# Attention ahead of two expert layers on one core: queries loaded ahead of values in three buffers, a unit's exponents in one instruction, routed transposes on four banks

## The chip, the cores and the metric

The kernel runs on one core of a Trainium2 chip. The metric is device time in microseconds (us), as the median of several runs. Engines are named as in the profile: PE multiplies matrices (PEld loads its weights), DVE, ACT and POOL work on vectors, SP issues most of the transfers (DMAs). Each engine takes its instructions in the order in which the program was written; a waiting instruction holds everything behind it on that engine.

## The reference

Three layers follow one another: attention (2 batches, 8 heads, 768 positions, 64 wide; each query sees a window of 31 keys and 24 block summaries), an expert layer in which every token goes through all 8 experts (weights from Sinkhorn), and one in which each token goes to a single expert.

```python
k_sum = k.reshape(B, H, nb, block, D).max(axis=3)
v_sum = v.reshape(B, H, nb, block, D).mean(axis=3)
scores_l = scale * np.matmul(q, k.transpose(0, 1, 3, 2))
mask_l = np.abs(pos[:, None] - pos[None, :]) < window
scores_s = scale * np.einsum('bhsd,bhnd->bhsn', q, k_sum) + np.log(block)
scores_all = np.concatenate([np.where(mask_l, scores_l, -1e9), scores_s], axis=-1)
a = np.exp(scores_all - np.max(scores_all, axis=-1, keepdims=True))
a = a / (np.sum(a, axis=-1, keepdims=True) + 1e-09)
attn = np.matmul(a, np.concatenate([v, v_sum], axis=2))
...
for e in range(E):                       # dense: every expert sees every token
    out += P[:, e:e + 1] * (np.maximum(x @ w1[e], 0.0) @ w2[e])
...
for e in range(E):                       # routed: a token goes to its best expert
    h = np.maximum(x[mask] @ w1[e], 0.0)
    out[mask] = gate_w[mask, None] * eom[mask, e, None] * (h @ w2[e])
```

## The kernel before

**Units.** Attention is cut into 16 units: a batch b, a half g of its positions (384 queries) and a pair hp of heads. The loop of `steps` runs 18 times; its step i carries out, in the order of the table `STEPS`, one part each of several units: `flip` of unit i-2 (PE transposes the finished weights `e`, L276, and ACT copies them out as `aT`), `scores` of unit i (PE, L220), `transposes_q` of unit i+1 (PE, L97), `means` of i-1, `maxima` of i (DVE: six pairs of instructions at L236 add the mask, write `e` to SBUF and leave the extreme of every row in `mx`), `fill_v` of i-1 (ACT), `exponents` of i (ACT, L249: six instructions of 120 columns, each with a bias from `mx` and a running sum into `sm`), `sum_v` of i (POOL, L128, three additions over the values `vn`), `transposes_k` of i+2 (PE, copies on DVE at L186, a reduction at L190), `apply` of i-2 (PE L289, then DVE makes `xhi`, `xlo`), and at the end `normalise` of i: DVE L258 and L259 turn `sm` into `rs`, POOL multiplies `e` by it (L261, 128x720). Then the step issues loads: a piece of the experts' weights (`raw`, the fillers), keys, queries, values.

**What sets the order.** The instructions of an engine stand as the Python code emits them. PE's first instruction of a step is `flip` of unit i-2, whose `e` was normalised at the end of step i-2: a whole step lies between. The function `merge` puts pieces of the dense layer's matmuls (L603, L623, with `hhi` on ACT and `hlo`, `acc` on DVE) between the parts of the attention from the end of step 6 on; before that attention runs alone, with `warm` matmuls on ones in its first steps. The weights of the dense layer arrive as `raw`; ACT makes `hi` of them (L471) and DVE `lo` (L472, both inputs in SBUF).

**Buffers.** `qn` (queries as loaded) has two buffers, `vn` one, `kn` three. Values of unit i+1 can only be loaded when `sum_v` of unit i is through. Loads of q, k and v all stand in SP's one queue. `whole` says for which head pairs the load takes each head apart, in longer runs; PE then transposes them with six 64-wide matmuls in place of three of 128.

**Routed part.** At the end, tiles of 128 tokens go through `flip_x`, `mm1`, `flip_h` and `mm2` (L1735 to L1772). `flip_h` writes two halves of `h`, transposed, into PSUM banks of role "t", which `flip_x` uses too; there are two such banks. `evac` empties one with ACT (`hi`) and then DVE (`lo`, L1728).

Of the kernel before, what the change touches and what calls it, by code (L numbers as in the profile page):

```python
# [12 lines left out]
ACTF = mybir.ActivationFunctionType  # L13
ALU = mybir.AluOpType
AX = mybir.AxisListType
# [7 lines left out]
class Attention:  # L23
# [10 lines left out]
    LAG = 2  # L34
    STEPS = (
        ("flip", -LAG, 0.65), ("scores", 0, 0.9), ("transposes_q", 1, 0.35),
        ("means", -1, 0.2), ("maxima", 0, 0), ("fill_v", -1, 0), ("exponents", 0, 0),
        ("sum_v", 0, 0), ("transposes_k", 2, 0.7), ("apply", -LAG, 0.95), ("normalise", 0, 0),
    )

    def __init__(self, tc, pool, ident, ones, masks, q, k, v, xhi, xlo, psum):
# [19 lines left out]
    def load_rows(self, src, n, tag, whole, bufs):  # L61

        p = src.shape[1] // n
        shape = [p, 2, n, 64] if whole else [p, n, 2, 64]
        t = self.pool.tile(shape, F32, tag=tag, name=tag, bufs=bufs)
        self.nc.sync.dma_start(  # L70
            out=t, in_=src.rearrange("h (p r) d -> p h r d" if whole else "h (p r) d -> p r h d", r=n)
        )
        return t
# [5 lines left out]

    def load_q(self, b, g, hp):  # L80
        self.qn[b, g, hp] = self.load_rows(
            self.q[b, 2 * hp:2 * hp + 2, 384 * g:384 * g + 384], 3, "qn", self.whole(b, g, hp), 2
        )

    def whole(self, b, g, hp):
        return b == g == 0 and hp < 2

    def transpose_rows(self, tr, rows, r0, whole):
        for r in range(3):
            if whole:  # L90
                for h in range(2):
                    self.nc.tensor.matmul(
                        tr[64 * h:64 * h + 64, r, :], rows[:, h, r0 + r], self.ident,
                        start=True, stop=True,
                    )
            else:
                self.nc.tensor.transpose(  # L97
                    tr[:, r, :], rows[:, r0 + r].rearrange("p h d -> p (h d)"), self.ident
                )
# [128 lines left out]
    def maxima(self, b, g, hp):  # L228
        nc = self.nc
        e, mx, sm = self.an[b, g, hp]  # L230
        for par in range(2):
            sc = self.sc[par]
            for j in range(3):
                qt = 3 * g + j
                m = 0 if qt == 0 else (2 if qt == 5 else 1)
                nc.vector.tensor_tensor_reduce(  # L236
                    out=e[:, par, j], in0=sc[:, j], in1=self.masks[:, m], scale=1.0,
                    scalar=3.0e38, op0=ALU.add, op1=ALU.min,
                    accum_out=mx[:, 3 * par + j:3 * par + j + 1],
                )  # L240

    def exponents(self, b, g, hp):
        e, mx, sm = self.an[b, g, hp]
        for par in range(2):
            if par:
                yield
            for j in range(3):
                i = 3 * par + j
                self.nc.scalar.activation(  # L249
                    out=e[:, par, j], in_=e[:, par, j], func=ACTF.Exp, scale=-1.0,  # L250
                    bias=mx[:, i:i + 1], accum_out=sm[:, i:i + 1],
                )

    def normalise(self, b, g, hp):
        nc = self.nc
        e, _, sm = self.an[b, g, hp]
        rs = self.pool.tile([128, 6], F32, tag="rs", name="rs", bufs=2)
        nc.vector.tensor_scalar(out=sm, in0=sm, scalar1=1.0e-9, scalar2=None, op0=ALU.add)  # L258
        nc.vector.reciprocal(rs, sm)  # L259
        an = e.rearrange("p a j c -> p (a j) c")  # L260
        nc.gpsimd.tensor_tensor(  # L261
            out=an, in0=an,
            in1=rs.unsqueeze(2).to_broadcast([128, 6, 120]), op=ALU.mult,
        )
        self.an[b, g, hp] = an
# [41 lines left out]
    def steps(self, fillers):  # L307

        U, LAG = self.units, self.LAG
        once = ("transposes_k", "means")

        def load(f, i):
            if i < len(U):
                f(*U[i])

        load(self.load_k, 0)
        load(self.load_q, 0)  # L320
        self.make_blocks()
        load(self.load_k, 1)
        load(self.load_q, 1)
        load(self.load_k, 2)
        load(self.load_vn, 0)
        load(self.load_v, 0)
        load(self.load_v, 1)
        self.warm(8)
        yield -LAG
        for _ in self.transposes_k(*U[0]):  # L330
            yield -LAG
        self.transposes_q(*U[0])
        for _ in self.transposes_k(*U[1]):
            yield -LAG
        load(self.load_k, 3)
        load(self.load_q, 2)
        load(self.load_vn, 1)
        yield -LAG
        for i in range(len(U) + LAG):
            parts = [  # L340
                (getattr(self, what), U[i + d], cost if U[i + d][1] == 0 or what not in once else 0)
                for what, d, cost in self.STEPS if 0 <= i + d < len(U)
            ]
            total, at = sum(p[2] for p in parts), 0
            for f, unit, cost in parts:
                n = 0
                for _ in f(*unit) or ():
                    n += 1
                    if cost:
                        yield i - LAG + (at + cost * n / 2) / total  # L350
                at += cost
                if cost and at < total:
                    yield i - LAG + at / total
            if i < 3 + LAG:
                self.warm(8)
            for f in fillers.get(i, ()):
                f()
            load(self.load_k, i + 4)
            load(self.load_q, i + 3)
            load(self.load_vn, i + 2)  # L360
            load(self.load_v, i + 2)
            yield i - LAG + 1
# [24 lines left out]
class DenseMoe:  # L387
# [56 lines left out]
    def load(self, which, hx, c):  # L444
        nc = self.nc
        e, f0 = hx // 2, 512 * (hx % 2)
        t = self.rpool.tile([128, 512], F32, tag="raw", name="raw", bufs=4)
        if self.strassen(hx):

            if which == 1:  # L450
                d, f = 256 * (c % 2), f0 + 256 * (c // 2)
                src = self.w1[e][d:d + 256, f:f + 256]
            else:
                f, d = f0 + 256 * (c // 2), 256 * (c % 2)
                src = self.w2[e][f:f + 256, d:d + 256]
            (nc.gpsimd if hx > self.FIRST else nc.sync).dma_start(
                out=t.rearrange("p (k f) -> p k f", k=2),
                in_=src.rearrange("(k p) f -> p k f", p=128),
            )
        elif which == 2:  # L460
            nc.sync.dma_start(out=t, in_=self.w2[e][f0 + 128 * c:f0 + 128 * c + 128, :])
        else:
            f = f0 + 128 * c
            nc.sync.dma_start(
                out=t.rearrange("p (k f) -> p k f", k=4),
                in_=self.w1[e][:, f:f + 128].rearrange("(k p) f -> p k f", p=128),
            )
        self.raw[which, hx, c] = t
# [1370 lines left out]
def kernel(  # L1839
# [14 lines left out]
    nc = tc.nc  # L1854
# [16 lines left out]
            "zX": (3, 5), "zY": (2,), "zD": (1,),  # L1871
        },
        "routed": {"a": (4,), "b": (5,), "t": (0, 1), "m2": (3, 2), "m1": (6, 7)},
    }
    phase = ["attention"]
    turn = {}
# [14 lines left out]
    def pool(stack, name, side):  # L1891
        return stack.enter_context(
            tc.tile_pool(name=name, bufs=1, side=side, reuse_waits="tile")
        )

    with ExitStack() as stacks:
# [38 lines left out]
        moe2 = RoutedMoe(tc, ident, routing, moe2_w1, moe2_w2, out, psum)  # L1935
# [110 lines left out]
        def until(what):  # L2046
            while what not in finished:
                next(late, None)
# [3 lines left out]
        until("early")  # L2052
        tail_stack.close()
        moe2.begin_rest(pool(tail_stack, "m2b", "right"))
        for _ in moe2.steps(lambda: until("final")):
            next(late, None)


# [29 lines left out]
```

## Time and profile before

| | us |
|---|---|
| median of 3 runs (1327.66 to 1328.57) | 1328.5 |
| profiled execution | 1328.97 |
| its span | 1326.9 |
| PE busy | 1289.9 (97%) |
| DVE busy | 846.2 (64%) |
| ACT busy | 744.4 (56%) |
| POOL busy | 341.9 (26%) |

The span is the time from the first to the last recorded instruction; 2.1 us of the profiled execution's time lie around it. A busy share is a mean over stages; what holds a stage is read from the rows of that stage, by the idle time in front of an instruction and by what ended it.

### The profile page before, as it was taken

What the parts mean: (1) busy time and instruction counts of PE and PEld (TensorE: products, weight loads), DVE (VectorE), ACT (ScalarE), POOL (GpSimd) and SP (SyncE); (2) the same over time, 40 slices, a digit from 0 to 9 for tenths busy, and PEclk for the clock granted to TensorE, in tenths of its full rate; (3) what the DMA queues carried; (4) which work ended last, traced back from release to release, by engine and by line L of the source; (5) the groups of instructions that cost most, each with busy time, mean ns of one, the idle gap of its engine ahead of it and who ended that gap; (6) DMA issues with size and microseconds to landing.
All of it is one profiled execution on the core that took longest, in us unless ns stands there. A gap on an engine that the chain in (4) does not pass through costs nothing. (4 is left out here: it accounts for less than half of the span.)

```text
span 1326.9 us, 27071 instructions
## 1 busy us (share of the span) xinstructions
PE 1289.9 (97%) x10067; PEld 1214.2 (92%) x10067; DVE 846.2 (64%) x1673; ACT 744.4 (56%) x1523; POOL 341.9 (26%) x365
## 2 busy tenths in 40 slices
PE   7899999999999999999999999999999999999995
PEld 7788789999999999999999999999999998788783
DVE  5764587687778787787777786787643358313440
ACT  4875223577677676677677676777632115234451
POOL 4351004333233242333233242332210001111110
PEclk8999999999999999999999999999999999999998
DMA  8761227589789897988898897987661236123440
GB/s 186 163 145 34 95 96 270 176 175 207 190 175 196 194 206 170 224 169 211 189 192 186 188 197 186 216 169 184 94 167 40 80 129 213 49 82 118 168 147 23
DMA packets 167278, 208.90 MB, mean 157 GB/s; under 512 B 52319, under 2 KB 100447, under 8 KB 167136
## 3 DMA queue, kind: packets, MB, share of 16 engines
q1 hardware_dynamic: 118288, 138.36, 33.5%
q0 software_dynamic: 48848, 68.70, 30.2%
q8 instruction: 82, 1.34, 0.4%
q14 instruction: 60, 0.49, 0.1%
HBM read 151.18 MB, written 56.62 MB: 157 GB/s over the span
## 5 line engine op out<-in xcount | busy, mean ns | idle before, releaser
L840 POOL DMA_DIRECT2D x2d<-acc x144 | 172.8, 1242 | 454.0 <-ACT acc L835 214.0
L676 PE MATMUL bank<-hi,hlo 128*128 128x256 f32 x672 | 190.0, 283 | 0.3 <-DVE hlo L711 0.3
L676 PE MATMUL bank<-lo,hhi 128*128 128x256 f32 x672 | 189.9, 283 | 0.0
L676 PE MATMUL bank<-hi,hhi 128*128 128x256 f32 x672 | 189.5, 282 | 0.0
L676 PE MATMUL bank<-Tlo,hi 128*128 128x256 f32 x576 | 162.9, 283 | 0.0
L676 PE MATMUL bank<-Thi,lo 128*128 128x256 f32 x576 | 162.6, 282 | 0.0
L676 PE MATMUL bank<-Thi,hi 128*128 128x256 f32 x576 | 162.1, 281 | 0.0
L676 PE MATMUL bank<-hi,acc 128*128 128x256 f32 x672 | 133.7, 282 | 0.0
L676 PEld LDWEIGHTS bank<-hi,hhi 128*128 128x128 f32 x672 | 127.9, 190 | 0.3 <-DVE acc L860 0.2
L676 PEld LDWEIGHTS bank<-hi,hlo 128*128 128x128 f32 x672 | 127.4, 190 | 0.5 <-DVE hlo L711 0.5
L676 PEld LDWEIGHTS bank<-lo,hhi 128*128 128x128 f32 x672 | 127.4, 190 | 0.0
L676 PE MATMUL bank<-xhi,hi 128*128 128x256 f32 x432 | 121.4, 281 | 0.7 <-ACT t L770 0.7
L676 PE MATMUL bank<-xlo,hi 128*128 128x256 f32 x432 | 121.4, 281 | 0.0
L676 PE MATMUL bank<-xhi,lo 128*128 128x256 f32 x432 | 121.3, 281 | 0.0
L676 PEld LDWEIGHTS bank<-hi,acc 128*128 128x128 f32 x672 | 109.8, 190 | 0.0
L676 PEld LDWEIGHTS bank<-Thi,hi 128*128 128x128 f32 x576 | 109.0, 189 | 0.0
L676 PEld LDWEIGHTS bank<-Thi,lo 128*128 128x128 f32 x576 | 108.6, 189 | 0.0
L676 PEld LDWEIGHTS bank<-Tlo,hi 128*128 128x128 f32 x576 | 108.3, 188 | 0.0
L711 DVE TENSOR_TENSOR hlo<-t,hhi 128x512 fp32r<-128x512 f32 x144 | 97.0, 685 | 14.2 <-ACT hhi L703 13.4
L703 ACT CAST hhi<-t 128x512 fp32r<-128x512 f32 x144 | 88.1, 619 | 23.7 <-DVE t L805 17.3
L610 ACT ACTIVATE hhi<-bank 128x384 fp32r<-128x384 f32 x64 | 31.4, 491 | 120.3 <-PE bank L603 120.1
L835 ACT ACTIVATE acc<-acc,P 128x256 f32<-128x256 f32 x216 | 96.7, 502 | 3.5 <-DVE acc L877 2.7
(311 smaller groups left out, 3463.4 us busy)
## 6 DMA issues: line engine op xcount, KB each, us to landing
x2d<-acc POOLq DMA_DIRECT2D x147, 256.0 KB, 5.1
Thi<-td SPq DMA_DIRECT2D x144, 256.0 KB, 3.6
Tlo<-td SPq DMA_DIRECT2D x144, 256.0 KB, 4.0
raw<-in_moe_w_dram POOLq DMA_DIRECT2D x88, 256.0 KB, 6.0
raw<-in_moe_w_dram SPq DMA_DIRECT2D x20, 1024.0 KB, 6.4
raw<-in_moe_w_dram SPq DMA_DIRECT2D x40, 256.0 KB, 3.9
x2d<-acc SPq DMA_DIRECT2D x21, 256.0 KB, 2.4
kn<-in_k_dram SPq DMA_DIRECT2D x8, 384.0 KB, 4.7
```

The costliest lines, as they stand in the source:

```text
L610: nc.scalar.activation(out=hhi[:, c], in_=ps, func=ACTF.Relu)
L676: self.nc.tensor.matmul(bank[:, 256 * f:256 * f + 256], x[:, o:o + 128], y[:, k], start=first and n == 1, stop=n == 12, skip_group_check=True,
L703: nc.scalar.copy(hi, src)
L711: nc.vector.tensor_tensor(out=lo, in0=src, in1=hi.bitcast(F32), op=ALU.subtract)
L835: nc.scalar.activation(out=out[:, s], in_=src[:, s], func=ACTF.Copy, scale=self.P[:, i, hx // 2:hx // 2 + 1],)
L840: nc.gpsimd.dma_start(out=self.sums[n:n + 256, 256 * dh:256 * dh + 256].rearrange("(c p) d -> p c d", p=128), in_=out.rearrange("p (c d) - ...
```

## The change

`normalise` moves from the end of step i to step i+1, right after `maxima`, and now makes the sums itself (a DVE reduction over `e`). `maxima` ends with a POOL instruction that subtracts `mx` from all of `e`, and `exponents` is one ACT instruction over the whole unit. `qn` gets three buffers, queries are loaded one unit earlier, and in a step's loads they stand ahead of the weights, keys and values. All four head pairs of the first half of batch 0 are loaded head by head. In the routed part the role "t" gets banks 0, 1, 4 and 5 from the point "final" on.

```diff
     STEPS = (
         ("flip", -LAG, 0.65), ("scores", 0, 0.9), ("transposes_q", 1, 0.35),
-        ("means", -1, 0.2), ("maxima", 0, 0), ("fill_v", -1, 0), ("exponents", 0, 0),
-        ("sum_v", 0, 0), ("transposes_k", 2, 0.7), ("apply", -LAG, 0.95), ("normalise", 0, 0),
+        ("means", -1, 0.2), ("maxima", 0, 0), ("normalise", -1, 0), ("fill_v", -1, 0),
+        ("exponents", 0, 0), ("sum_v", 0, 0), ("transposes_k", 2, 0.7), ("apply", -LAG, 0.95),
     )
...
-            self.q[b, 2 * hp:2 * hp + 2, 384 * g:384 * g + 384], 3, "qn", self.whole(b, g, hp), 2
+            self.q[b, 2 * hp:2 * hp + 2, 384 * g:384 * g + 384], 3, "qn", self.whole(b, g, hp), 3
...
     def whole(self, b, g, hp):
-        return b == g == 0 and hp < 2
+        return b == g == 0
...
+        an = e.rearrange("p a j c -> p (a j) c")
+        nc.gpsimd.tensor_tensor(
+            out=an, in0=an, in1=mx.unsqueeze(2).to_broadcast([128, 6, 120]), op=ALU.subtract
+        )
 
     def exponents(self, b, g, hp):
-        e, mx, sm = self.an[b, g, hp]
-        for par in range(2):
-            if par:
-                yield
-            for j in range(3):
-                i = 3 * par + j
-                self.nc.scalar.activation(
-                    out=e[:, par, j], in_=e[:, par, j], func=ACTF.Exp, scale=-1.0,
-                    bias=mx[:, i:i + 1], accum_out=sm[:, i:i + 1],
-                )
+        e, _, _ = self.an[b, g, hp]
+        self.nc.scalar.activation(out=e, in_=e, func=ACTF.Exp, scale=-1.0)
...
+        nc.vector.tensor_reduce(out=sm, in_=an, axis=AX.X, op=ALU.add)
         nc.vector.tensor_scalar(out=sm, in0=sm, scalar1=1.0e-9, scalar2=None, op0=ALU.add)
         nc.vector.reciprocal(rs, sm)
...
         load(self.load_k, 2)
+        load(self.load_q, 2)
         load(self.load_vn, 0)
...
         load(self.load_k, 3)
-        load(self.load_q, 2)
+        load(self.load_q, 3)
         load(self.load_vn, 1)
...
+            load(self.load_q, i + 4)
             for f in fillers.get(i, ()):
                 f()
             load(self.load_k, i + 4)
-            load(self.load_q, i + 3)
...
         "routed": {"a": (4,), "b": (5,), "t": (0, 1), "m2": (3, 2), "m1": (6, 7)},
+        "slots": {"t": (0, 1, 4, 5), "m2": (3, 2), "m1": (6, 7)},
...
-        for _ in moe2.steps(lambda: until("final")):
+
+        def ready():
+            until("final")
+            phase[0] = "slots"
+
+        for _ in moe2.steps(ready):
```

On POOL, from the end of step 0 to the end of step 1 of the attention loop, the order before is this (L261 is the multiplication that ends `normalise`, L128 the three additions of `sum_v`, L150 clears part of a buffer for values):

```order
L261 TENSOR_TENSOR e<-e,rs 128x720
L150 MEMSET vw 32x128
L128 TENSOR_TENSOR vn<-vn 96x2x256
L128 TENSOR_TENSOR vn<-vn 96x2x128
L128 TENSOR_TENSOR sv<-vn 96x128
L261 TENSOR_TENSOR e<-e,rs 128x720
```

And now, in step 1 (L242 is the subtraction, L258 the multiplication):

```order
L242 TENSOR_TENSOR e<-e,mx 128x720
L258 TENSOR_TENSOR e<-e,rs 128x720
L128 TENSOR_TENSOR vn<-vn 96x2x256
L128 TENSOR_TENSOR vn<-vn 96x2x128
L128 TENSOR_TENSOR sv<-vn 96x128
L150 MEMSET vw 32x128
```

The multiplication of a unit has moved behind the subtraction of the next unit, which needs that unit's `maxima`; the additions over the values now follow both.

On DVE, after the maxima of step 10 (L236 is their last pair), the order before is this (L296 and L297 take the result of `apply` apart, L633 adds to the dense layer's output):

```order
L236 ISA mx 128x1
L296 CAST xhi_112<-bank_1428 128x384
L297 TENSOR_TENSOR xlo_114<-bank_1428,xhi_112 128x384
L258 TENSOR_SCALAR sm<-sm 128x6
L259 RECIPROCAL rs<-sm 128x6
L633 COPY acc_107<-bank_1456 128x512
```

And now:

```order
L236 ISA mx 128x1
L255 TENSOR_REDUCE sm<-e 128x6
L256 TENSOR_SCALAR sm<-sm 128x6
L257 RECIPROCAL rs<-sm 128x6
L293 CAST xhi_112<-bank_1414 128x384
L294 TENSOR_TENSOR xlo_114<-bank_1414,xhi_112 128x384
L631 COPY acc_107<-bank_1438 128x512
```

The reciprocal has moved ahead of `xhi` and `xlo` and belongs to the unit before; a reduction over that unit's 720 columns is new. PE's own rows stand in the order of before, apart from the transposes of the head pairs that are now loaded head by head.

On SP, from the last keys loaded ahead of the loop, the loads of before are these:

```order
L70 DMA kn<-in_k_dram 128x12x64
L70 DMA qn<-in_q_dram 128x6x64
L70 DMA vn<-in_v_dram 96x2x512
L464 DMA raw<-in_moe_w_dram 128x4x128 x4
L70 DMA qn<-in_q_dram 128x6x64
L70 DMA vn<-in_v_dram 96x2x512
```

And now:

```order
L70 DMA kn<-in_k_dram 128x2x384
L70 DMA qn<-in_q_dram 128x2x192
L70 DMA vn<-in_v_dram 96x2x512
L70 DMA qn<-in_q_dram 128x6x64
L462 DMA raw<-in_moe_w_dram 128x4x128 x4
L70 DMA vn<-in_v_dram 96x2x512
```

The queries shown are those of units 2 and 3 before and of units 3 and 4 now; the second of them has moved ahead of the four pieces of weights.

## Rows read from the trace of the kernel before

**Rows 1.** Windows: stretch, its length, busy time (instructions) by engine, granted clock, DMA share, GB/s.

```profile
14.00:26.00 12.00, 6.38 (x61) 6.22 (x49) 5.28 (x21) 4.80 (x17) 4.88 (x8) 0.72 0.99 215
58.00:121.00 63.00, 62.92 (x921) 55.56 (x918) 41.29 (x175) 47.38 (x158) 25.59 (x30) 1.00 0.49 115
```

**Rows 2.** Waits of PE: us in total, times, longest us.

```profile
PE bank L97 <- DMA qn<-in_q_dram: 6.9, 2, 5.6
PE bank L97 <- DVE mx L236: 4.0, 2, 2.7
PE bank L1772 <- DVE xtlo L1728: 2.9, 5, 1.0
```

**Rows 3.** Timeline of PE, first transposes of step 7: start, length, [idle before and releaser].

```profile
57.75 0.38 PE L276 MATMUL bank<-ident,e 128*120 128x128 f32 x2
```

**Rows 4.** One load of weights on SP's queue, with its landing.

```profile
L461 SPq DMA_DIRECT2D raw<-in_moe_w_dram x1: 386/386/386, 27.9 to 27.9; - x1
...
DMA to landing us min/median/max: 3.0/3.0/3.0
```

**Rows 5.** Timeline of ACT and of DVE, what step 3's maxima follow.

```profile
31.82 0.60 ACT L471 CAST hi<-raw 128x512 fp32r<-128x512 f32 x1
...
32.76 2.34 DVE L472 TENSOR_TENSOR lo<-raw,hi 128x512 fp32r<-128x512 f32 x2 [0.34 <-ACT hi L471]
```

**Rows 6.** PE in step 5: a flip (timeline), and the scores alone (window of L220).

```profile
43.08 0.82 PE L276 MATMUL bank<-ident,e 128*120 128x128 f32 x6
...
43.00:45.66 2.66, 1.04 (x48) 0.94 (x48) 1.00 0.78 185
```

**Rows 7.** Timeline of DVE: first of the maxima of steps 7, 9, 10, 12, 13, 14.

```profile
60.31 0.27 DVE L236 CUSTOM_DVE_ANT_0 e<-bank,masks 128x120 f32<-128x120 f32 x1
...
72.06 0.27 DVE L236 CUSTOM_DVE_ANT_0 e<-bank,masks 128x120 f32<-128x120 f32 x1
...
81.25 0.27 DVE L236 CUSTOM_DVE_ANT_0 e<-bank,masks 128x120 f32<-128x120 f32 x1
...
95.01 0.27 DVE L236 CUSTOM_DVE_ANT_0 e<-bank,masks 128x120 f32<-128x120 f32 x1
...
103.34 0.27 DVE L236 CUSTOM_DVE_ANT_0 e<-bank,masks 128x120 f32<-128x120 f32 x1
...
111.46 0.27 DVE L236 CUSTOM_DVE_ANT_0 e<-bank,masks 128x120 f32<-128x120 f32 x1
```

**Rows 8.** Timeline of PE: first transposes of steps 8, 10, 11, 13, 14, 15.

```profile
63.66 0.38 PE L276 MATMUL bank<-ident,e 128*120 128x128 f32 x2
...
75.81 0.38 PE L276 MATMUL bank<-ident,e 128*120 128x128 f32 x2
...
82.73 0.38 PE L276 MATMUL bank<-ident,e 128*120 128x128 f32 x2
...
97.92 0.38 PE L276 MATMUL bank<-ident,e 128*120 128x128 f32 x2
...
106.02 0.38 PE L276 MATMUL bank<-ident,e 128*120 128x128 f32 x2
...
112.70 0.38 PE L276 MATMUL bank<-ident,e 128*120 128x128 f32 x2
```

**Rows 9.** All multiplications of `normalise` (ns min/median/max); one on the timeline.

```profile
L261 POOL TENSOR_TENSOR e<-e,rs x16: 1390/1392/1908, 15.2 to 119.7; 128x720 f32<-128x720 f32 x16
...
59.13 0.19 DVE L259 RECIPROCAL rs<-sm 128x6 f32<-128x6 f32 x1
59.24 0.69 DVE L472 TENSOR_TENSOR lo<-raw,hi 128x512 fp32r<-128x512 f32 x1
...
59.50 1.68 POOL L261 TENSOR_TENSOR e<-e,rs 128x720 f32<-128x720 f32 x1 [6.50 <-DVE rs L259]
```

**Rows 10.** DVE: one unit's maxima (window of L236); the reductions over keys (ns).

```profile
60.31:61.65 1.34, 1.29 (x12) 1.00 0.91 174
...
L190 DVE TENSOR_REDUCE ks<-kT x8: 952/953/954, 7.1 to 75.2; 128x24 f32<-128x768 f32 x8
```

More of the change, by code (lines that the diff above doesn't have):

```diff
@@ L257, in normalise @@
         rs = self.pool.tile([128, 6], F32, tag="rs", name="rs", bufs=2)
+        an = e.rearrange("p a j c -> p (a j) c")
+        nc.vector.tensor_reduce(out=sm, in_=an, axis=AX.X, op=ALU.add)
         nc.vector.tensor_scalar(out=sm, in0=sm, scalar1=1.0e-9, scalar2=None, op0=ALU.add)
         nc.vector.reciprocal(rs, sm)
-        an = e.rearrange("p a j c -> p (a j) c")
         nc.gpsimd.tensor_tensor(
```

## The prediction

> **What bounds the kernel now.** I began with windows along the span. Between 58 and 121 us, where pieces of the dense layer lie between the parts of the attention, PE is busy 62.92 of 63 us [rows 1]: whatever holds PE there lengthens the span by its whole length, since no idle time follows that could take it up. Ahead of that, attention runs alone, and PE has holes: 6.38 of 12 us from 14 to 26, at a mean granted clock of 0.72 [rows 1]. Then I asked what ended PE's waits. Line L97, the transposes of queries, carries most of it: 6.9 us put down to the queries' loads and 4.0 to the maxima [rows 2]. L97 reads only queries and the identity and the maxima write neither, so I count the second row as queries too: 10.9 us in four waits, the largest gain on offer. A third row, 2.9 us at L1772, is the second half of `flip_h` waiting for a PSUM bank that `xtlo` empties [rows 2]; it belongs to the four banks. Last I read where the first transposes of each step stand against the maxima of the step before, because the change ties the two together.
>
> **The new tie.** Before, a unit's multiplication on POOL was issued a step earlier than its flip needed it. Now it stands in POOL's queue behind the subtraction of the next unit, which waits for that unit's maxima. The flip is PE's first instruction of a step, and in order, so all matmuls behind it (scores, and the dense layer's pieces) wait with it. From the first of a unit's maxima to the next step's flip there now lie: the maxima, 1.29 us [rows 10]; a hop from DVE to POOL, 0.18 (the reciprocal ends at 59.13 + 0.19, the multiplication starts at 59.50) [rows 9]; the subtraction, which no trace shows, but which has the shape, type and broadcast operand of the multiplication, so 1.39; the multiplication, 1.39 [rows 9]; and a hop to PE, which I put at the same 0.18. Sum: 4.43 us.
>
> The bounds of the two POOL instructions are the fastest and the slowest of the 16 multiplications, 1.39 and 1.91 [rows 9]. The long ones had DVE's `lo` beside them (0.69 us at 59.24 under the 1.68 one) [rows 9]. After the maxima DVE now has a reduction of 720 columns, at most the 0.95 us of the one over 768 [rows 10], then the two small instructions, `xhi` and `xlo`, so `lo` mostly comes behind the multiplication: I take the low end. [...]
>
> **Steps 7 to 15, where PE is full.** The room that the trace leaves is the distance from a step's first maxima [rows 7] to the next step's flip [rows 8]: step 7, 63.66 - 60.31 = 3.35; step 9, 3.75; step 10, 1.48; step 12, 2.91; step 13, 2.68; step 14, 1.24. Of the three not shown, step 8 has 3.08, steps 11 and 15 have 5.06 and 4.51, enough. What lacks to 4.43 is a stall: 1.08, 1.35 and 0.68 in steps 7 to 9, together 3.1; 2.95, 1.52, 1.75 and 3.19 in steps 10, 12, 13, 14, together 9.4. I add them up. They add if the maxima's start is set by PE, as then each stall moves the next maxima too; DVE is busy only 41.29 of the 63 us [rows 1], so it is mostly waiting for others there. Sum **+12.5**.
>
> **Steps 0 to 6, attention alone.** The four waits for queries go: those of unit 2 are on the way ahead of all values, and from then on each load is one unit further ahead, with a third buffer. But flips are then held by the tie, one step after another: flip 0.82, scores 1.04 [rows 6], a hop 0.18, and 4.43: 6.47 us a step. And the first weights of the dense layer still stand on SP behind the values of unit 2, whose single buffer waits for POOL's `sum_v` of unit 1, which now comes behind a subtraction and a multiplication. So I leave their landing at 27.9 + 3.0 = 30.9 [rows 4]. ACT's `hi` takes 0.60 and DVE's two `lo` between 2 x 0.69 [rows 9] and 2.34 [rows 5], and the maxima of step 3 stand behind them on DVE: 32.9 to 33.8, and flip of step 4 at 37.3 to 38.3. I take 37.5, nearer to the low end since the one ACT instruction frees ACT before the landing. Three steps of 6.47 give step 7 at 56.9, where the trace has 57.75 [rows 3]: **-0.8**, not -10.9. (With the upper end, 0; if step 4 begins 3 us earlier, -4.)
>
> **The other edits.** The loads head by head double the 64-wide matmuls of a few units ahead of step 4, in PE's holes: nothing, unless the holes were gone. One ACT instruction in place of six: ACT is done sooner but starts later, behind POOL; what hangs on `e` is the next step's reduction, over a step later: nothing. The reduction sits on DVE while the subtraction runs on POOL, shorter than that: nothing. With four banks in turn, the second half of `flip_h` no longer takes the bank that `flip_x` has just filled: of 2.9 us [rows 2] I take 2.5, since its matmuls then wait for the same `xtlo` a little later as an input: **-2.5** (bounds 0 and -2.9).
>
> **Sum.** -0.8 + 12.5 - 2.5 = +9.2 us. Against the profiled execution, 1328.97, that is 1338.2; against the median of 1328.5, which is 0.5 lower, 1337.7. About 0.2% (2.7 us) is what a measurement here can tell from no change.
>
> **Rivals.**
> Loads were the price (faster). The tie does not bind because the maxima come early enough everywhere: with queries there, PE reaches the scores sooner and DVE, not full, follows. Then the 10.9 and the 2.5 are gained whole: 1315.1; half of the queries' gain and no stall is 1320.5. It decides whether step 7's flip starts before about 47 (57.75 - 10.9) and whether the later flips show no wait for POOL. Against it: the room of 1.24 and 1.48 in steps 14 and 10, far below 4.43. Chance 0.15.
>
> Stalls that do not add (no change): a stall lets ACT and DVE catch up, later maxima come earlier against PE, and only the largest of each stretch counts, 1.35 and 3.19: -0.8 + 4.5 - 2.5 = +1.2, 1329.7. Chance 0.18.
>
> POOL held by DVE (slower still): both POOL instructions at 1.91 in steps 3 to 9, where `lo` runs, a tie of 5.47. Step 4's flip at 38.5 and three steps of 7.51 put step 7 at 61.0, +3.3; stalls 2.12, 2.39, 1.72 make 6.2; with 9.4 and -2.5: +16.4, 1344.9. The row of 1.68 beside `lo` speaks for it [rows 9], the order after the maxima against. [...] Chance 0.12.
>
> Queries late all the same (the change does not do what it says): on SP they still stand behind values that wait for `sum_v` (its order is in the section on the change), so step 7 is no earlier: 12.5 - 2.5 = +10.0, 1338.5, hardly to be told from my forecast by time. Chance 0.07.
>
> **How the numbers follow.** My forecast, 1332 to 1342 about 1337.7, has 0.48. Slower: 0.48 + 0.12 + 0.07 = 0.67. Same: 0.18. Faster: 0.15. The range runs from 1327, the low side of "stalls do not add", to 1345, the POOL rival: it leaves out the 0.15 and a little above.
>
> **What would show it.** Right: in the windows, PE no longer full between 58 and 121, some 12 us idle; in PE's waits, flips released by POOL's multiplication, longest about 3, in steps 10 and 14; no wait of more than a microsecond at L97 for queries; step 7's flip near 57; the waits at `flip_h` for `xtlo` gone. On POOL, subtraction and multiplication back to back, 1.39 each. Wrong: a flip that follows its multiplication by microseconds of other work, step 7 below 50, or multiplications of 1.9.

## The result, and the profile after

The changed kernel takes 1346.1 us (median of 4 runs, 1345.2 to 1346.7) against 1328.2: the ratio is 1.0136, with a 95% interval from 1.0121 to 1.0151. That is 17.9 us slower, where 9.2 slower were forecast; 1346.1 lies just above the range that was given, 1327 to 1345. The profiled spans, 1344.9 and 1326.9, differ by 18.0 us, so the two traces account for the whole of it.

PE's waits in the changed kernel (us in total, times, longest) answer to [rows 2]:

```profile
PE bank L273 <- POOL e L258: 18.0, 14, 3.5
PE bank L92 <- DMA kn<-in_k_dram: 3.0, 1, 3.0
PE bank L139 <- POOL sv L128: 2.9, 3, 1.0
...
PE bank L1770 <- DVE xtlo L1726: 0.2, 1, 0.2
```

Flips released by POOL's multiplication now stand first, with 18.0 us; no wait for queries is left, and the wait for a bank of the routed transposes fell from 2.9 to 0.2. The 3.0 us for keys and the 2.9 for `sv` are new; they lie ahead of step 5.

The windows of [rows 1], again, in the changed kernel:

```profile
14.00:26.00 12.00, 8.19 (x98) 7.42 (x88) 7.03 (x20) 3.67 (x6) 7.51 (x10) 0.72 0.80 203
58.00:121.00 63.00, 53.54 (x747) 45.45 (x745) 46.74 (x151) 29.06 (x51) 32.09 (x35) 0.97 0.51 117
```

PE was full from 58 to 121 us and is now idle for 9.5 of the 63 us there; its mean granted clock is 0.97, not 1.00. To see where the time went I cut both spans at the first transposes of step 7 and at the end of the last `apply`. First the kernel before, then, in the second fence, the changed one:

```profile
57.75:129.31 71.56, 71.17 (x1000) 62.48 (x998) 43.91 (x180) 50.47 (x164) 25.68 (x30) 1.00 0.43 102
129.31:1326.90 1197.59, 1174.22 (x8360) 1110.78 (x8359) 768.65 (x1368) 656.86 (x1239) 291.56 (x283) 1.00 0.65 160
```

```profile
60.71:151.09 90.38, 76.33 (x999) 64.30 (x999) 57.76 (x190) 37.07 (x65) 37.31 (x39) 0.96 0.35 80
151.09:1344.90 1193.81, 1174.14 (x8360) 1110.69 (x8359) 767.92 (x1368) 655.92 (x1239) 291.40 (x283) 1.00 0.65 160
```

Step 7 begins 2.96 us later, steps 7 to 17 take 18.8 us longer, and the rest is 3.8 us shorter: 2.96 + 18.8 - 3.8 = 18.0.

The timeline of PE has the flips' waits one by one (idle before and releaser in brackets); these answer to [rows 3, 8]:

```profile
32.40 0.87 PE L273 MATMUL bank<-ident,e 128*120 128x128 f32 x6 [0.62 <-POOL e L258]
...
52.80 1.31 PE L273 MATMUL bank<-ident,e 128*120 128x128 f32 x6 [3.51 <-POOL e L258]
...
60.71 0.87 PE L273 MATMUL bank<-ident,e 128*120 128x128 f32 x6 [0.25 <-POOL e L258]
...
92.77 0.87 PE L273 MATMUL bank<-ident,e 128*120 128x128 f32 x6 [2.97 <-POOL e L258]
...
131.64 1.53 PE L273 MATMUL bank<-ident,e 128*120 128x128 f32 x6 [3.27 <-POOL e L258]
```

These are the flips of steps 3, 6, 7, 11 and 15. The six transposes at 131.64 take 1.53 us in place of 0.87: half clock. The windows of steps 6, 11 and 15, which begin behind the three longest holes, show it in the clock column:

```profile
52.80:60.71 7.91, 7.66 (x100) 6.69 (x100) 4.59 (x18) 4.00 (x7) 3.04 (x4) 0.78 0.74 160
...
92.77:102.61 9.84, 9.84 (x107) 8.32 (x108) 4.94 (x19) 3.98 (x7) 5.64 (x7) 0.83 0.44 112
...
131.64:141.53 9.89, 9.51 (x102) 7.79 (x102) 5.32 (x19) 2.97 (x5) 2.78 (x2) 0.83 0.01 2
```

Shorter windows have clocks of 0.50 and 1.00; for each step, one inside the slow stretch and one behind it:

```profile
53.30:56.30 3.00, 3.00 (x55) 2.61 (x54) 0.28 (x3) 0.96 (x2) 0.00 (x0) 0.50 0.59 129
56.80:60.71 3.91, 3.66 (x43) 3.08 (x41) 3.81 (x12) 2.94 (x5) 2.84 (x3) 1.00 0.87 185
94.20:97.20 3.00, 3.00 (x48) 2.17 (x50) 0.69 (x1) 0.01 (x1) 1.19 (x3) 0.50 0.23 63
97.70:102.61 4.91, 4.91 (x47) 4.38 (x47) 4.22 (x18) 3.12 (x5) 3.10 (x3) 1.00 0.63 147
131.64:135.00 3.36, 3.36 (x11) 2.97 (x12) 0.00 (x0) 1.78 (x3) 0.00 (x0) 0.50 0.02 5
135.00:141.53 6.53, 6.15 (x92) 4.81 (x91) 5.32 (x19) 1.18 (x2) 2.78 (x2) 1.00 0.00 1
```

An estimate from these two values: a mean of 0.83 over 9.84 us is 2 x 0.17 x 9.84 = 3.3 us at half clock, in which PE does 1.7 us of work less than at full clock; the other two windows give 3.5 and 3.4.

Last the tie itself, in step 10, on DVE and on POOL:

```profile
88.17 0.27 DVE L236 CUSTOM_DVE_ANT_0 e<-bank,masks 128x120 f32<-128x120 f32 x1
...
89.38 0.90 DVE L255 TENSOR_REDUCE sm<-e 128x6 f32<-128x720 f32 x1
90.31 0.65 DVE L256 TENSOR_SCALAR sm<-sm 128x6 f32<-128x6 f32 x1
90.99 0.19 DVE L257 RECIPROCAL rs<-sm 128x6 f32<-128x6 f32 x1
...
89.54 1.39 POOL L242 TENSOR_TENSOR e<-e,mx 128x720 f32<-128x720 f32 x1 [4.22 <-DVE mx L236]
91.33 1.39 POOL L258 TENSOR_TENSOR e<-e,rs 128x720 f32<-128x720 f32 x1 [0.40 <-DVE rs L257]
```

The maxima begin at 88.17, the multiplication ends at 92.72 and the flip starts at 92.77: the tie is 4.60 us. It is 4.6 to 4.7 in steps 7 to 14, except in step 11, where PE is busy up to the next flip. Both POOL instructions take 1.39, but there is a hole of 0.40 us between them, since the reciprocal is late. It is late because the addition of 1e-9 to six sums a row, 128x6, takes 0.65 us. Over all units:

```profile
L256 DVE TENSOR_SCALAR sm<-sm x16: 171/711/861, 16.9 to 145.4; 128x6 f32<-128x6 f32 x16
```

It ends when the subtraction on POOL does (90.96 and 90.93), and so in all 15 units that have a subtraction beside it, 0.02 to 0.03 us after it; in the last unit, with none beside it, it takes 0.17.

### The profile page after: what moved, and what is told of

It reads as the page before. It is cut to its first block, busy times and chain, and to the rows that moved or that the text cites. A ratio compares the mean times of both kernels' runs of the same rounds, so it can differ in the third digit from the quotient of the medians.

```text
span 1344.9 us, 27022 instructions
## 1 busy us (share of the span) xinstructions
PE 1299.4 (97%) x10121; PEld 1218.4 (91%) x10121; DVE 867.2 (64%) x1689; ACT 719.9 (54%) x1347; POOL 363.1 (27%) x381
```

## The experiments

My theory: the loss is the tie (maxima, subtraction, multiplication, flip), where it is longer than the room, with the half clock that follows the longest holes. Rivals: the added work on POOL and DVE costs by itself; the loads make the start late. Each run was timed beside the kernel before, whose median in these series lay between 1326.6 and 1327.4. A difference from the changed kernel is therefore taken between the two ratios to before; by their intervals it is good to about 3 us.

### Normalise ahead of the maxima

```diff
-        ("means", -1, 0.2), ("maxima", 0, 0), ("normalise", -1, 0), ("fill_v", -1, 0),
+        ("means", -1, 0.2), ("normalise", -1, 0), ("maxima", 0, 0), ("fill_v", -1, 0),
```

> The changed kernel with normalise of the unit before put ahead of maxima, not behind it: the same instructions, only DVE's reduction and reciprocal and POOL's multiplication come before the next unit's maxima and subtraction. Theory (the tie): flips are no longer released by the multiplication, the 12 to 14 us of such waits in steps 7 to 15 and the two late half-clock stretches go; 1322 to 1328 us. Rival (the added work itself, a subtraction on POOL and a reduction on DVE, costs): 1338 or more, DVE or POOL full. Rival (the loads cost, keys behind queries): step 7 still 3 us late, and 1331 to 1334 us.

Measured: 1332.3 us, ratio to before 1.0037 (1.0024 to 1.0051). By the ratios 13 us came back, but not all: the time misses the forecast of 1322 to 1328. It lies in the range of the loads' rival (1331 to 1334), but not by that rival's way: step 7 begins at 58.95, 1.2 us later than before [rows 3] and not 3, while from the flip of step 7 to that of step 17 it takes 6.3 us longer. Step 10 on DVE, POOL and PE shows what is left:

```profile
83.92 0.56 DVE L609 SCALAR_TENSOR_TENSOR hlo<-bank,hhi 128x384 fp32r<-128x384 f32 x1 [2.51 <-ACT hhi L608]
84.40 0.89 DVE L255 TENSOR_REDUCE sm<-e 128x6 f32<-128x720 f32 x1
85.32 0.17 DVE L256 TENSOR_SCALAR sm<-sm 128x6 f32<-128x6 f32 x1
...
85.87 1.39 POOL L258 TENSOR_TENSOR e<-e,rs 128x720 f32<-128x720 f32 x1 [4.08 <-DVE rs L257]
...
87.31 0.87 PE L273 MATMUL bank<-ident,e 128*120 128x128 f32 x6 [1.28 <-POOL e L258]
```

The reduction still stands behind the dense layer's `hlo`, which waits for ACT; the multiplication comes at 85.87 and the flip at 87.31, 1.28 us late. The tie is shorter, not cut. The addition takes 0.17 us here, with no POOL instruction beside it.

### Normalise at the end of its own unit's step

```diff
-        ("means", -1, 0.2), ("maxima", 0, 0), ("normalise", -1, 0), ("fill_v", -1, 0),
-        ("exponents", 0, 0), ("sum_v", 0, 0), ("transposes_k", 2, 0.7), ("apply", -LAG, 0.95),
+        ("means", -1, 0.2), ("maxima", 0, 0), ("fill_v", -1, 0), ("exponents", 0, 0),
+        ("sum_v", 0, 0), ("transposes_k", 2, 0.7), ("apply", -LAG, 0.95), ("normalise", 0, 0),
```

> The changed kernel with normalise back at the end of its own unit's step, subtraction, one exponent instruction, loads and banks as changed. Theory (the tie, through POOL's queue and through DVE's: in the kernel with normalise ahead of the maxima the reciprocal still stood behind hlo on DVE): no flip waits for the multiplication, steps 7 to 17 take 72 to 75 us as before the change, 1322 to 1328 us. Rival (the added reduction and subtraction cost by themselves, DVE being full in steps 7 to 9 and ahead of them): 1330 to 1336 and DVE full.

Measured: 1324.9 us, ratio to before 0.9980 (0.9970 to 0.9989): some 21 us better than the changed kernel by this one move, with all of its other edits left in. The flips' waits for POOL come down to one, and PE is nearly full again from 58 to 121 us:

```profile
PE bank L273 <- POOL e L258: 0.9, 1, 0.9
```

```profile
58.00:121.00 63.00, 61.60 (x863) 53.09 (x860) 46.74 (x176) 32.18 (x57) 36.02 (x39) 1.00 0.48 112
```

This is the run that decides for the tie.

### New exponents and moved normalise alone

The changed kernel's `STEPS`, `maxima`, `exponents` and `normalise` in the kernel before; old loads and banks (the edits are those of the diff above).

> The kernel before with the new exponents and the moved normalise alone, loads and banks as before. Theory (the tie): at least the 18.8 us that steps 7 to 17 lost in the changed kernel, and the start not earlier than there: 1347 to 1352. Rival (the loads had a share in the loss): 1340 or less.

Measured: 1353.3 us, ratio 1.0190 (1.0168 to 1.0212), 26.2 us slower by the medians, and just above the expected range of 1347 to 1352; the flips' waits (17.9 us, 13 times) are those of the changed kernel. The other edits are thus worth some 7 us here and 3.6 alone (the run with loads and banks together, below); with runs from 1348 to 1355 that difference is not shown.

### New exponents, normalise left at the end

```diff
-        ("means", -1, 0.2), ("maxima", 0, 0), ("normalise", -1, 0), ("fill_v", -1, 0),
...
+        ("sum_v", 0, 0), ("transposes_k", 2, 0.7), ("apply", -LAG, 0.95), ("normalise", 0, 0),
```

(on the kernel of the last experiment)

> The kernel before with the subtraction on POOL, the one exponent instruction and the reduction, but normalise at the end of its own unit's step; old loads and banks. Theory (the added work is not the loss, the tie is): within 1.5 us of before, 1326 to 1329. Rival (the work of 1.39 us on POOL and 0.9 on DVE a unit costs by itself): 1331 or more.

Measured: 1329.9 us, ratio 1.0022 (1.0013 to 1.0031), 2.8 us slower than before: between theory (1326 to 1329) and rival (1331 or more). The added work does cost a little. Its windows and its waits:

```profile
58.00:76.00 18.00, 16.65 (x270) 14.48 (x262) 17.66 (x63) 9.25 (x17) 11.26 (x12) 1.00 0.65 138
```

```profile
PE bank L97 <- DMA qn<-in_q_dram: 12.2, 7, 5.6
```

DVE is full (17.66 of 18 us), PE is no longer, and with the old loads the waits for queries grew from four to seven. 26.2 - 2.8 = 23.4 us are the tie's in this pair (22 by the ratios).

### Old exponents, normalise moved behind the maxima

```diff
-        ("means", -1, 0.2), ("maxima", 0, 0), ("fill_v", -1, 0), ("exponents", 0, 0),
-        ("sum_v", 0, 0), ("transposes_k", 2, 0.7), ("apply", -LAG, 0.95), ("normalise", 0, 0),
+        ("means", -1, 0.2), ("maxima", 0, 0), ("normalise", -1, 0), ("fill_v", -1, 0),
+        ("exponents", 0, 0), ("sum_v", 0, 0), ("transposes_k", 2, 0.7), ("apply", -LAG, 0.95),
```

> The kernel before with normalise alone moved behind the next unit's maxima; exponents with bias and running sum as before, no subtraction, no reduction, old loads and banks. Theory (what lacks between a tie and the room becomes stall): the tie is now 1.29 maxima + 0.36 sum and reciprocal + two hops of about 0.2 + 1.39, 3.3 to 3.5 us; against the rooms of the trace (3.35, 3.08, 1.48, 2.91, 2.68, 1.24) it lacks 0.1, 0.4, 2.0, 0.6, 0.8, 2.2: 6 us, and 0 to 2 at the start: +6 to +8, with less or no loss of clock as the holes are shorter. 1333 to 1336. Rival (only the subtraction ahead of the multiplication makes flips wait): under 2 us, below 1330.

Measured: 1332.9 us, ratio 1.0044 (1.0025 to 1.0062), 5.8 us slower, just under the 6 to 8 that the rule gave. The flips wait where, and nearly as long as, room and tie say (the tie is 3.2 here; 3.2 - 1.48 = 1.7 and 3.2 - 1.24 = 2.0):

```profile
85.86 0.87 PE L276 MATMUL bank<-ident,e 128*120 128x128 f32 x6 [1.56 <-POOL e L261]
...
118.90 0.87 PE L276 MATMUL bank<-ident,e 128*120 128x128 f32 x6 [1.82 <-POOL e L261]
```

After these holes of 1.6 and 1.8 us the clock stayed at 1.00. Step 10 also has a wait of 1.84 us for queries, at 80.07, which the kernel before does not have: not all of the 5.8 us is the tie's.

### Matmuls on ones in the holes ahead of steps 11 and 15

```diff
             total, at = sum(p[2] for p in parts), 0
+            if i in (11, 15):
+                self.warm(16)
```

> The changed kernel with 16 matmuls on ones added as the first PE work of steps 11 and 15, in the holes of 2.97 and 3.27 us ahead of those flips. Theory (each hole was followed by 3.4 us at half clock, in which PE did 1.7 us less): the clock stays full after both, 3.4 us less: 1342 to 1343.5. Rival (the lower clock hides in other waits): 1345.5 to 1347.

Measured: 1342.5 us, ratio to before 1.0113 (1.0097 to 1.0128), 3 us less than the changed kernel by adding work, with an interval that only just leaves out zero; the trace shows it more sharply. The matmuls lie in the hole and the clock of the steps behind stays full:

```profile
88.28 3.73 PE L302 MATMUL bank<-ones 128*128 128x128 f32 x32
91.85 0.82 PE L273 MATMUL bank<-ident,e 128*120 128x128 f32 x6
```

```profile
91.85:100.14 8.29, 8.29 (x110) 7.18 (x109) 4.96 (x19) 3.97 (x7) 5.21 (x7) 1.00 0.47 124
129.30:137.60 8.30, 7.91 (x105) 6.41 (x103) 5.32 (x19) 2.87 (x5) 2.78 (x2) 1.00 0.01 3
```

The same steps took 9.84 and 9.89 us in the changed kernel: 3.1 us more.

### Reduction and reciprocal ahead of the maxima, multiplication behind the subtraction

```diff
-("maxima", 0, 0), ("normalise", -1, 0),
+("sums", -1, 0), ("maxima", 0, 0), ("normalise", -1, 0),
```

(`sums` holds the three DVE instructions of `normalise`)

> The changed kernel with the reduction, the sum and the reciprocal ahead of the maxima, the multiplication where the change put it, behind the subtraction. Theory (the 0.40 us hole between subtraction and multiplication is DVE's reduction, late behind the maxima): tie 4.25 in place of 4.65, the hole gone, 4 to 6 us less: 1340 to 1342.5. Rival (the hole is a fixed price between POOL instructions): no change, 1346.

Measured: 1349.9 us, ratio to before 1.0163 (1.0147 to 1.0178), 3 to 4 us slower than the changed kernel: a miss. The hole on POOL did go. But where the maxima wait behind `hlo`, the three instructions now stand between `hlo` and the maxima, 1.25 us that had lain beside the subtraction:

```profile
86.22 0.56 DVE L615 SCALAR_TENSOR_TENSOR hlo<-bank,hhi 128x384 fp32r<-128x384 f32 x1 [3.36 <-ACT hhi L614]
86.69 0.89 DVE L255 TENSOR_REDUCE sm<-e 128x6 f32<-128x720 f32 x1
87.62 0.17 DVE L256 TENSOR_SCALAR sm<-sm 128x6 f32<-128x6 f32 x1
...
87.94 0.24 DVE L236 CUSTOM_DVE_ANT_0 e<-bank,masks 128x120 f32<-128x120 f32 x1
...
89.28 1.39 POOL L242 TENSOR_TENSOR e<-e,mx 128x720 f32<-128x720 f32 x1 [5.45 <-DVE mx L236]
90.62 1.39 POOL L264 TENSOR_TENSOR e<-e,rs 128x720 f32<-128x720 f32 x1
```

Step 12, at full clock in both, takes 9.45 us in place of 8.69. The longer holes cost clock as well: those ahead of steps 11 and 15 are 3.74 and 4.04 us here, and the mean clock of these steps is 0.76 and 0.71, not 0.83. The addition is 0.17 us again. That set the next question: is it the work on DVE that is late, or this one instruction?

### Without the addition

```diff
-        nc.vector.tensor_scalar(out=sm, in0=sm, scalar1=1.0e-9, scalar2=None, op0=ALU.add)
```

> The changed kernel without the addition of 1e-9 to the sums (L256), which it leaves out; the reciprocal follows the reduction at once. Theory (the addition, 128x6, takes 0.65 to 0.86 us beside the subtraction and 0.17 elsewhere: it is held until POOL's subtraction is through, and with it the reciprocal and the multiplication): the reciprocal, 0.19 us wherever it stood, is done before the subtraction ends, the 0.40 us hole ahead of the multiplication goes, the tie is 4.25, 4 to 6 us less over some 12 ties: 1340 to 1342.5. Rival (any small DVE instruction is held there, the reciprocal too): hole of 0.35 to 0.4, 1345 to 1346.5. Rival (the reduction itself is what is late): hole of 0.2.

Measured: 1338.4 us, ratio to before 1.0086 (1.0064 to 1.0108), some 6.6 us less than the changed kernel (interval 3 to 10) for one instruction on 128x6. Reduction and reciprocal are done at 85.70, the multiplication follows the subtraction with no hole:

```profile
84.57 0.90 DVE L255 TENSOR_REDUCE sm<-e 128x6 f32<-128x720 f32 x1
85.51 0.19 DVE L256 RECIPROCAL rs<-sm 128x6 f32<-128x6 f32 x1
...
84.74 1.39 POOL L242 TENSOR_TENSOR e<-e,mx 128x720 f32<-128x720 f32 x1 [3.96 <-DVE mx L236]
86.08 1.39 POOL L257 TENSOR_TENSOR e<-e,rs 128x720 f32<-128x720 f32 x1
```

Only the addition had been held; the reciprocal, as small, was not, nor the reduction. From the flip of step 7 to that of step 17 the trace has 82.26 us in place of 86.65: 4.4 less, with most ties shorter by 0.4. Another 3.0 lie ahead of step 7. Half of that is step 6, which takes 6.25 us in place of 7.91: it keeps the full clock, though a hole of 3.08 us stands before it. That the addition's absence did this is not shown; of the same first steps two traces also differ (step 2 begins at 25.95 in the changed kernel, at 20.36 in the run with matmuls on ones).

### The other parts on the kernel before

Four banks alone (the changes to `banks` and `ready` of the diff):

> The kernel before with the four banks for the routed transposes alone. Theory: the 2.9 us of waits for a bank go, nothing else moves: -2.5 to -3.8 us, 1324.5 to 1325.8. Rival (the matmuls then wait for the same copies as inputs): under 1 us, 1327.5.

Measured: 1324.2 us, ratio 0.9979 (0.9970 to 0.9988), -2.9 us; the wait for `xtlo` is down to 0.2 us.

Loads alone (queries ahead, three buffers, all four pairs head by head):

> The kernel before with the queries ahead in three buffers and all four head pairs loaded head by head, exponents and banks as before. Theory (the tie is the whole loss, the loads help): the four waits of 10.9 us go but weights and DVE set the pace next, step 7 is 2 to 6 us earlier than 57.75: 1322 to 1326.5. Rival (the loads are what made the start late): step 7 at 58 or later, 1328 to 1331.

Measured: 1326.9 us, ratio 0.9996 (0.9987 to 1.0005): no change that can be told. Step 7 is 3.6 us earlier, as the theory had it, and step 10 only 0.8 (75.81 before [rows 8]):

```profile
54.14 0.38 PE L276 MATMUL bank<-ident,e 128*120 128x128 f32 x2
...
75.01 0.38 PE L276 MATMUL bank<-ident,e 128*120 128x128 f32 x2
```

The run with the banks alone, whose loads are the old ones, has 56.92 and 75.18 at these places, so two traces differ by 0.8 and 0.6 us without any change to the loads: the gain at step 7 is clear, that at step 10 is not. It is given back in steps 7 to 9. DVE is nearly full there in the kernel before, 17.31 us of 18.06. That it is what takes the gain back is my reading, and no run takes work off DVE there; in this run PE also waits 1.39 us for keys, at 72.23.

Loads and banks together:

> The kernel before with the loads and the banks, exponents and normalise as before. Theory (gains of separate stretches add): -0.2 and -2.9 together, 1323.5 to 1324.5. Rival (they overlap): 1325 to 1327.

Measured: 1323.7 us, ratio 0.9971 (0.9960 to 0.9981), -3.6 us.

The same with only two pairs head by head (`whole` as before):

> The kernel before with the queries ahead in three buffers and the four banks, but only two head pairs loaded head by head. Theory (the head by head loads of pairs 2 and 3 double PE's transposes ahead of step 4, in holes): within 1 us of the version with them, 1323 to 1325. Rival (the longer runs bring the keys sooner and are most of the loads' gain): 1325.5 to 1327. Rival (their 64-wide matmuls delay PE at the start): 1321 to 1322.5.

Measured: 1323.2 us, ratio 0.9977 (0.9966 to 0.9988). The two can't be told apart, nor from the banks alone: the longer runs of pairs 2 and 3 are worth nothing that shows. These versions and the one with normalise at the end all beat both kernels, at 1323 to 1325 us.

## Why the prediction was wrong

The direction and the mechanism were right: moving normalise behind the next unit's maxima costs more than all the rest gains, and taking that one move back gives some 21 us. The size was half. By the steps of the prediction:

**Steps 0 to 6: -0.8 forecast, +2.96 measured.** This step failed. I set step 4 at 37.5, from a load's landing, with three steps of 6.47 behind it. The flips of steps 2 to 7 start at 25.95, 32.40, 39.26, 46.12, 52.80 and 60.71. Step 4 is 1.8 late: in this trace the tie already holds the flips of steps 3 and 4, and the load came later too, as ACT's `hi` waited for it until 32.65. In the run with matmuls on ones, the same program up to there, step 4 does begin at 37.64, and step 7 at 59.85 all the same. So the three steps behind it are what failed in both. Steps 4 and 5 take 6.86 and 6.68, mostly by the hole of 0.40. Step 6 takes 7.91: the flip behind the hole of 3.51 us and the scores run at half clock (0.50 from 53.30 to 56.30 us), and the maxima come 3.2 us after the flip, not 2.0. I had priced no clock here either. Together 1.8 + 0.4 + 0.2 + 1.4 = 3.8.

**"The reduction sits on DVE while the subtraction runs on POOL, shorter than that: nothing".** This failed too. The reduction took 0.90, as bounded, but I left out the addition behind it, which is held until POOL's subtraction ends. I had the two engines hold one another in the wrong direction: as a rival in which DVE lengthens POOL's instructions, to 1.91. That did not come: all 32 took 1.38 to 1.39. The measured 1346.1 is near that rival's 1344.9, by another way. The trace has the addition at 0.17 us alone and at 0.65 to 0.86 beside a subtraction, whose end it outlasts by 0.02 to 0.03 us in 15 of 15 units, and the reduction at 0.89 to 0.90 us with or without one. Why the addition waits and the reduction does not, no run shows.

**Steps 7 to 10 and 12 to 14: +12.5 forecast, +14.4 measured** (from flip to flip, each against the same step before: 1.60, 1.65, 0.66, 3.17, 1.77, 2.05, 3.51). The rule held, step by step; the tie was 4.60 to 4.68 and not 4.43. In step 10 it was 4.43 + 0.40 for the hole, less 0.23 for the two hops, 0.08 to POOL and 0.05 to PE in place of 0.18 each: 4.60. The stalls do add: that rival is out.

**Not in the sum: the clock, most of +3.7.** Steps 11 and 15, for which I had no stall, take 1.57 and 2.17 us more. The longest holes of this stretch, 2.97 and 3.27 us, come just before them, and each was followed by about 3.4 us at a clock of 0.50, by the estimate above 1.7 us of work lost; the rest of step 15 is its tie of 4.95 against a room of 4.51. Rows of the kernel before showed a mean clock of 0.72 from 14 to 26 us [rows 1], and I didn't carry that to the holes I forecast; behind the wait of 5.62 us that ends at 20.01, its trace has 0.50 up to 24 us (first line), and 1.00 from 25 us on. The run with matmuls on ones takes 3.1 us out of these two steps. Steps 16 and 17 add 0.7.

```profile
19.00:24.00 5.00, 3.99 (x19) 4.02 (x20) 1.98 (x3) 2.93 (x10) 2.45 (x3) 0.50 1.19 264
25.00:28.00 3.00, 3.00 (x72) 2.67 (x72) 1.88 (x12) 1.95 (x6) 2.04 (x2) 1.00 0.75 187
```

**Banks: -2.5 forecast, -2.9 alone**, and 3.8 in the last stretch of the trace against 2.9 us of waits; part of that difference between two traces is outside the transposes.

**Queries.** The waits are gone, as forecast, and as forecast the 10.9 us were not on offer; the loads alone show no change. "Queries late all the same" is out, and so is "the tie does not bind".

The sum of what I missed: 3.8 at the start, 1.9 in the stalls, 3.7 and 0.7 behind them, less 1.3 at the end: 8.8, of 17.9 - 9.2 = 8.7.

## What to carry to other kernels

When a step is moved, write down for each waiting engine the whole chain from its new input to its consumer, with every small instruction in it, and set it against the room that the trace leaves at that place; where the engine that waits is full, what lacks is lost, place by place (here 14.4 us in seven steps), and a loop of such ties starts at the first place where it binds. A hole behind which PE's clock falls costs more than its length (here 3.1 us more for two of them), so a forecast stall needs the clock's price beside it, read from holes of the same kernel. A change of several parts hides its one bad part: here the place of one entry in a table cost some 21 us, while all the other edits together, with that entry left in its place, gained 2.

## What the runs showed of the hardware

- A DVE addition of 128x6 waited for a POOL instruction of 1.39 us: 0.17 us alone, 0.65 to 0.86 beside it, and its end came 0.02 to 0.03 us after POOL's in 15 of 15 units. The reduction over 128x720 and the reciprocal of 128x6 beside the same POOL instruction did not wait (0.90 and 0.19 us in all). Leaving the addition out took 4.4 us from steps 7 to 16.
- Holes of 2.97 and 3.27 us on a PE that was full before were followed by about 3.4 us at half clock (0.50); holes of 1.56 to 1.83 us were not (1.00). Without the addition the holes at the same places were 2.53 and 2.83 us, and the mean clock from 58 to 121 us, where the first of them lies, was 0.97 again, while step 6, behind a hole of 3.08 us, kept the full clock (6.25 us in place of 7.91): the length of a hole alone does not tell. Filling the two holes with matmuls that nobody needs took 3.1 us from the steps behind them.
